# Batch 3 of a sliding-window attention moved into the steady pattern: scores, spread and values in other places of groups 1 and 2

## The chip, the cores and the metric

The kernel runs on one core of a Trainium2 chip. The metric is the device time of one execution in microseconds (us). Five engines take part, each with its own queue of instructions: TensorE (PE), VectorE (DVE), ScalarE (ACT), GpSimd (POOL) and SyncE (SP, which only issues transfers here).

## What is computed

Eight batches of eight heads of causal attention over 576 positions with a window of 128 and a linear distance bias, and then, over all 4608 tokens, a gated feed-forward block:

```python
scores = scale * np.matmul(q, k.transpose(0, 1, 3, 2))
...
mask = (rel >= 0) & (rel < window)
scores = np.where(mask, scores + bias[None], -1000000000.0)
...
attn = np.exp(scores)
attn = attn / (np.sum(attn, axis=-1, keepdims=True) + 1e-09)
return np.matmul(attn, v).astype(np.float32)
...
g = x @ w_gate
gelu = 0.5 * g * (1.0 + erf(g * inv_sqrt2))
val = x @ w_val
return (gelu * val @ w_out).astype(np.float32)
```

The head dimension is 64, the model width 512, the inner width 1536. Inputs and output are float32; the kernel works in bf16 with float32 sums.

## The kernel before

Two kinds of work are woven together. The attention goes batch by batch (`b`, 0 to 7, 576 tokens each), the feed-forward block group by group (`g`, 0 to 8, 512 tokens each). Batch `b` writes its columns of `xT`, the transposed attention output, which the groups read. Group `g` ends at token 512(g+1), so a group needs batches up to `g` or `g + 1`: group 3, tokens 1536 to 2047, needs the end of batch 2 and most of batch 3.

A batch passes through these steps. Heads are taken in four pairs (`c`), the 576 query positions in two parts (`s`, of 320 and 256 columns).

- `load` (L95): GpSimd issues five transfers for each of q, k and v, into `qs`, `ks` and `vb`, of which there are two each (batch parity).
- `transposes_dma` (L167): SP issues two DMA transposes, `kT<-ks` and `qT<-qs`.
- `scores2`, `scores` (L174): products of keys and queries on PE, exponentials on ACT (L181) into `P`, and a product with the mask `emask` on DVE (L184). `scores` works on two of the four head pairs at a time; its exponentials take four PSUM buffers of `ps`.
- `sums` (L232): PE adds up the probabilities with a matrix of ones; DVE takes the reciprocals (L241) into `r`.
- The reciprocals are spread over the partitions into `rb`, in one of two ways. `spread_pe` (L255): four float32 products with a selection matrix on PE for each part, and four copies (L262), two on ACT and two on DVE. `spread_dma` (L245, L247): SP writes `r` to DRAM (`rd`) and reads it back twice with a broadcast (`rb<-rd`).
- `values` (L273): products of values and probabilities on PE; DVE multiplies by `rb` and writes `xT` (L279).

A group has a gate phase of twelve steps `gate_val` (L292, GELU on ACT in L296, product on DVE in L297) and an out phase of eight steps `out_half` (L308), the numbers 0 to 7 in the lists below; the odd ones end with a copy on ACT (L313) and a transfer from SP (L315).

Every engine runs its instructions in the order in which the code issues them. The order is written out by hand: a list `todo[g]` for the out phases of groups 0 to 2, and the function `steps` for the later ones. In the lists, `("s", b, s, cs)` is a call of `scores`, `"s2"` of `scores2`, `"sum"` of `sums`, `"spread"` of `spread_pe`, and `"pv"` of `values`.

In groups 3 to 6 there is a steady pattern for batch `g + 1`: its sums and `spread_dma` come after the first gate step, its values after gate steps 8 and 10; in the out phase, the scores of batch `g + 2` come ahead of and between the products, the last of them ahead of step 6. SP then issues, in the order of the code, rd, two rb, the two transposes of batch `g + 2`, and the four outputs. Batches 0 to 3 are handled in the out phases, with `spread_pe`; batches 2, 3 and 4 are transposed by DMA at the start of groups 1 and 2.

PSUM has eight buffers `ps` of 128x512 float32, from one pool (`bank`), which gate steps, out steps, scores, sums, spreads and values share. `P` has eight buffers for part 0 and four for part 1. `gelu` has three buffers, `r` and `rb` one each.

Of the kernel before, what the change touches and what calls it, by code (L numbers as in the profile page):

```python
# [26 lines left out]
def kernel(  # L27
# [11 lines left out]
    B, H, S, D = q.shape  # L39
# [27 lines left out]
    def bank():  # L67
        ps = psum.tile([128, 512], FP32, name="ps")
        for _ in range(heat.pop()):
            nc.tensor.matmul(out=ps, lhsT=zeros[:, 0:128], rhs=zeros, start=True, stop=True)  # L70
        heat.append(0)
        return ps
# [26 lines left out]
    def load_qk(b):  # L99
        load(qs[b % 2], q, b)  # L100
        load(ks[b % 2], k, b)
# [18 lines left out]
    def load_v(b):  # L120
        load(vb[b % 2], v, b)
# [28 lines left out]
    def transpose(b, what, c, copy):  # L150
        ps = bank().bitcast(BF16)
        for j in range(5):
            nc.tensor.transpose(  # L153
                out=ps[:, 128 * j:128 * j + 128],
                in_=(qs, ks)[what][b][:, j, 128 * c:128 * c + 128], identity=ident)
        copy(out=(qT, kT)[what][b][:, :, c, :],  # L156
             in_=ps[:, 0:640].rearrange("p (j t) -> p j t", t=128))
# [7 lines left out]
    def transposes_dma(b):  # L165
        for src, dst in ((ks, kT), (qs, qT)):
            nc.sync.dma_start_transpose(  # L167
                out=dst[b % 2].rearrange("p j c t -> p (j c) t"),
                in_=src[b % 2].rearrange("p j x -> p (j x)"))
# [49 lines left out]
    def prob(b, s, c, i, j, n):  # L219
        if (s, j) == (0, 2):  # L220
            return probs2[b][:, c, i, 0:n]
        return probs[b, s, c][:, i, PCOL[s][j]:PCOL[s][j] + n]
# [3 lines left out]
    def sums(b, s):  # L226

        ps = bank()
        for j, a, e in PIECES[s]:
            for i in (0, 1):  # L230
                for c in range(4):
                    nc.tensor.matmul(  # L232
                        out=ps[32 * c:32 * c + 32, a:e],
                        lhsT=ones[:, min(j, 1), i, :], rhs=prob(b, s, c, i, j, e - a),
                        start=(i == 0 and j == 2 * s), stop=(i == 1 and j == 2 * s + 2),
                        skip_group_check=True)
        if s == 0:
            sumrow[b] = r_pool.tile([128, S], FP32, name="r")
            recip[b] = r_pool.tile([128, 4, S], FP32, name="rb")
        lo, hi = PART[s]  # L240
        nc.vector.reciprocal(sumrow[b][:, lo:hi], ps[:, 0:hi - lo])  # L241

    def spread_dma(b):
        d = d_pool.tile([4, 2, S], FP32, name="rd")
        nc.sync.dma_start(out=d.rearrange("c i s -> (c i) s"), in_=sumrow[b][0:128:16, :])  # L245
        for i in (0, 1):
            nc.sync.dma_start(  # L247
                out=recip[b][64 * i:64 * i + 64, :, :],
                in_=d[:, i, :].unsqueeze(0).to_broadcast((64, 4, S)))
# [14 lines left out]
    def values(b, s, cs):  # L264
        lo, hi = PART[s]
        pss = []
        for c in cs:
            ps = bank()
            pss.append(ps)
            for j, a, e in PIECES[s]:  # L270
                for i in (0, 1):
                    h = 2 * c + i
                    nc.tensor.matmul(  # L273
                        out=ps[64 * i:64 * i + 64, a:e],
                        lhsT=vb[b % 2][:, j, 64 * h:64 * h + 64],
                        rhs=prob(b, s, c, i, j, e - a),
                        start=(j == 2 * s), stop=(j == 2 * s + 2), skip_group_check=True)
        for c, ps in zip(cs, pss):
            nc.vector.tensor_tensor(  # L279
                out=xT[:, c, b * S + lo:b * S + hi], in0=ps[:, 0:hi - lo],  # L280
                in1=recip[b][:, c, lo:hi], op=ALU.mult)
# [3 lines left out]
    def gate_val(g, f, lo=0, hi=512):  # L285
        if g not in hid:
            hid[g] = h_pool.tile([128, NF, 512], BF16, name="hT")
        t0 = 512 * g
        pg, pv = bank(), bank()
        for w, ps in ((wg, pg), (wv, pv)):  # L290
            for c in range(4):
                nc.tensor.matmul(  # L292
                    out=ps[:, 0:hi - lo], lhsT=w[:, c, 128 * f:128 * (f + 1)],
                    rhs=xT[:, c, t0 + lo:t0 + hi], start=(c == 0), stop=(c == 3))
        gl = g_pool.tile([128, 512], BF16, name="gelu")
        nc.scalar.activation(out=gl[:, 0:hi - lo], in_=pg[:, 0:hi - lo], func=AF.Gelu)  # L296
        nc.vector.tensor_tensor(out=hid[g][:, f, lo:hi], in0=pv[:, 0:hi - lo],  # L297
                                in1=gl[:, 0:hi - lo], op=ALU.mult)
# [3 lines left out]
    def out_half(g, u):  # L302
        t, half = u // 2, u % 2
        if half == 0:
            acc[g] = bank()
        po = acc[g]
        for f in range(6 * half, 6 * half + 6):
            nc.tensor.matmul(  # L308
                out=po, lhsT=hid[g][:, f, 128 * t:128 * (t + 1)],
                rhs=wo[:, f, :], start=(f == 0), stop=(f == NF - 1))  # L310
        if half == 1:
            osb = o_pool.tile([128, DM], FP32, name="osb")
            nc.scalar.copy(out=osb, in_=po)  # L313
            r0 = 512 * g + 128 * t
            nc.sync.dma_start(out=out[r0:r0 + 128, :], in_=osb)  # L315
# [93 lines left out]
    for t in (qs[0], ks[0]):  # L409
# [11 lines left out]
        1: [("s2", 2), ("s", 2, 0, (0, 1)), 0, ("s", 2, 0, (2, 3)), 1, 2,  # L421
            ("s", 2, 1, (0, 1), lambda: sums(2, 0)), 3, ("s", 2, 1, (2, 3)), ("s2", 3),
            ("spread", 2, 0), ("pv", 2, 0), 4, ("sum", 2, 1), ("s", 3, 0, (0, 1)), 5, 6,
            ("spread", 2, 1), ("pv", 2, 1), ("s", 3, 0, (2, 3)), 7],
        2: [("s", 3, 1, (0, 1), lambda: sums(3, 0)), 0, ("s", 3, 1, (2, 3)), 1,
            ("spread", 3, 0), ("pv", 3, 0), ("s2", 4), ("sum", 3, 1), 2,
            ("s", 4, 0, (0, 1)), 3, ("spread", 3, 1), ("pv", 3, 1), 4, ("s", 4, 0, (2, 3)), 5,
            ("s", 4, 1, (0, 1)), 6, 7, ("s", 4, 1, (2, 3))],
    }

    def steps(g):
        b = g + 2
        if g in todo:
            return todo[g]
        if b >= B:
            return range(8)
        return [("s2", b), ("s", b, 0, (0, 1)), 0, 1, ("s", b, 0, (2, 3)), 2, 3,
                ("s", b, 1, (0, 1)), 4, 5, ("s", b, 1, (2, 3)), 6, 7]

    RUN = {"s2": scores2, "s": scores, "sum": sums, "spread": spread_pe,  # L440
           "pv": lambda b, s: values(b, s, range(4))}

    for g in range(NG):
        for b in ((), (2, 3), (4,))[g] if g < 3 else ():
            transposes_dma(b)
        if g + 2 < B:
            load_v(g + 2)
        for f in range(3 if g == 0 else 0, NF):
            gate_val(g, f)
            if g == 0 and f >= 8:  # L450
                for w in (0, 1):
                    transpose(1, w, f - 8, (act, dve)[w])
            if 3 <= g < B - 1:
                if f == 0:
                    sums(g + 1, 0)
                    sums(g + 1, 1)
                    spread_dma(g + 1)
                    if g + 2 < B:
                        transposes_dma(g + 2)
                elif f in (8, 10):  # L460
                    for s in (0, 1):
                        values(g + 1, s, (f - 8, f - 7))
        if g + 3 < B:
            load_qk(g + 3)
        for item in steps(g):
            if isinstance(item, int):
                out_half(g, item)
            else:
                RUN[item[0]](*item[1:])
# [30 lines left out]
```

The softmax here doesn't subtract the row's maximum and nothing guards it: scores larger than these inputs give would overflow.

## Time and profile before

| | |
|---|---|
| time, median of 4 runs | 366.95 us (366.79 to 367.12) |
| profiled execution: time, span | 367.12 us, 365.4 us |
| PE busy | 351.3 us, 96% |
| DVE, ACT, POOL busy | 189.0, 187.3, 107.9 us |
| granted PE clock | 1.00 |
| gate phase of group 2 begins, by the PE timeline | 111.36 us |
| out phase of group 2 begins | 132.17 us |
| gate phase of group 3 begins | 151.57 us |
| gate phase of group 4 begins | 189.56 us |

The span is the time from the first to the last recorded instruction. Rows of the profile name the engine, the line of the kernel, the operation and, as out<-in, what it writes and reads; a row of a timeline starts with its start and its duration in us. PEld is the load of weights, which overlaps PE. SPq and POOLq are the queues from which SP and GpSimd issue transfers. Matmuls are pipelined, so the sum of their durations is no measure of how near PE is to its peak; the chain of waits tells what the end depended on.

### The profile page before, as it was taken

To read this page: it belongs to the slowest core of one execution; us is meant where nothing else is said; L and a number is where in the kernel's file an instruction comes from. 1 tells how busy PE (TensorE), PEld (TensorE's weight loads), DVE (VectorE), ACT (ScalarE), POOL (GpSimd) and SP (SyncE) were. 2 spreads that over 40 slices of the span, in tenths; PEclk is the share of its full clock that TensorE was granted. 3 is DMA by queue.
4 is the path that set the end of the run, shared out by engine and by line. 5 is a ranking of instruction groups with operands and counts; after the bars stand their busy time and mean duration, and the time that the engine had idled before them with its cause. 6 is when DMAs were issued, how large, how long until landed. Compare 5 with 4: busy or idle time off the path is not lost.

```text
span 365.4 us, 6652 instructions
## 1 busy us (share of the span) xinstructions
PE 351.3 (96%) x2638; PEld 170.7 (47%) x2682; DVE 189.0 (52%) x307; ACT 187.3 (51%) x339; POOL 107.9 (30%) x140
## 2 busy tenths in 40 slices
PE   7889999999999999999999999999999999999995
PEld 2455545444454445444544444444444444444442
DVE  4794448533795469474537554755564404302320
ACT  4953487435966376933783277436842223323321
POOL 8945869904419203900940040000000000000000
PEclk9999999999999999999999999999999999999999
DMA  9999999999989994999992992093205030011002
GB/s 103 138 200 178 183 157 188 175 160 201 142 120 122 132 96 81 154 101 227 112 198 45 220 104 90 31 216 58 88 31 131 0 111 5 0 60 58 0 31 86
DMA packets 151168, 41.41 MB, mean 113 GB/s; under 512 B 138816, under 2 KB 144448, under 8 KB 151136
## 3 DMA queue, kind: packets, MB, share of 16 engines
q0 software_dynamic: 112608, 18.88, 68.0%
q1 hardware_dynamic: 38528, 22.10, 27.8%
q8 instruction: 21, 0.34, 0.4%
q14 instruction: 11, 0.09, 0.1%
HBM read 42.47 MB, written 9.51 MB: 142 GB/s over the span
## 4 chain that ended last, share of the span: by engine, by line
PE 83%; ACT 6%; DMA 6%; DVE 2%; issue 1%; POOL 0%; SPq 0%; ACTq 0%; DVEq 0%; POOLq 0%
PE ps L292 48%; PE ps L308 23%; ACT P L181 5%; DMA qT<-qs 5%; PE ps L174 4%; PE ps L273 4%; PE ps L232 2%; PE ps L255 1%; DMA ks<-in_k_dram 1%; DVE xT L279 1%; DVE P L184 1%; PE ps L153 1%; DVE r L241 0%; ACT L181 0%; PE ps L70 0%
## 5 line engine op out<-in xcount | busy, mean ns | idle before, releaser
L297 DVE TENSOR_TENSOR hT<-ps,gelu 128x512 bf16<-128x512 f32 (+2 forms) x111 | 74.4, 674 | 121.6 <-PE ps L292 106.9
L296 ACT ACTIVATE gelu<-ps 128x512 bf16<-128x512 f32 (+2 forms) x111 | 64.9, 585 | 119.8 <-PE ps L292 119.7
L292 PE MATMUL ps<-xT,wg 128*128 128x512 bf16 (+2 forms) x430 | 110.9, 373 | 1.7 <-DVE xT L279 0.7
L292 PE MATMUL ps<-xT,wv 128*128 128x512 bf16 (+2 forms) x435 | 110.4, 373 | 0.6
L308 PE MATMUL ps<-wo,hT 128*128 128x512 bf16 x413 | 97.2, 380 | 1.5 <-issue 0.6
L181 ACT ACTIVATE P<-ps 128x512 bf16<-128x512 f32 x144 | 74.4, 633 | 7.1 <-PE ps L174 7.0
L292 PEld LDWEIGHTS <-wv 128*128 128x128 bf16 x444 | 43.3, 98 | 50.5 <-issue 0.5
L292 PEld LDWEIGHTS <-wg 128*128 128x128 bf16 x444 | 41.9, 98 | 49.8 <-issue 2.3
L184 DVE TENSOR_TENSOR P<-P,emask 128x1024 bf16<-128x1024 bf16 x72 | 48.3, 685 | 31.3 <-ACT P L181 31.0
L308 PEld LDWEIGHTS <-hT 128*128 128x128 bf16 x432 | 39.8, 98 | 49.0 <-issue 4.4
L95 POOL DMA_DIRECT2D vb<-in_v_dram x40 | 33.7, 869 | 77.4 <-PE ps L273 77.2
L313 ACT COPY osb<-ps 128x512 f32<-128x512 f32 x36 | 21.7, 603 | 37.5 <-PE ps L308 33.0
L95 POOL DMA_DIRECT2D qs<-in_q_dram x35 | 29.6, 884 | 24.7 <-DMA qT<-qs 13.0
L241 DVE RECIPROCAL r<-ps 128x320 f32<-128x320 f32 (+1 forms) x16 | 30.7, 1937 | 2.6 <-PE ps L232 2.6
L95 POOL DMA_DIRECT2D ks<-in_k_dram x35 | 29.7, 898 | 4.5 <-DMA wv<-in_moe_w_val_dram 1.6
L174 PE MATMUL ps<-qT,kT 64*128 64x256 bf16 (+1 forms) x384 | 23.3, 245 | 1.9 <-DVE kT L156 0.4
L279 DVE TENSOR_TENSOR xT<-ps,rb 128x320 bf16<-128x320 f32 (+1 forms) x64 | 24.7, 447 | 0.5 <-PE ps L273 0.3
L174 PEld LDWEIGHTS <-kT 64*128 64x128 bf16 x384 | 13.0, 94 | 16.7 <-issue 12.4
L273 PE MATMUL ps<-P,vb 128*64 128x128 bf16 (+2 forms) x384 | 18.4, 243 | 0.1
L273 PEld LDWEIGHTS <-vb 128*64 128x64 bf16 x384 | 14.7, 110 | 6.8 <-issue 6.8
L232 PE MATMUL ps<-P,ones 128*32 128x128 bf16 (+2 forms) x384 | 10.8, 243 | 1.3 <-DVE P L184 1.1
L232 PEld LDWEIGHTS <-ones 128*32 128x32 bf16 x384 | 7.9, 96 | 5.5 <-issue 4.7
(50 smaller groups left out, 98.2 us busy)
## 6 DMA issues: line engine op xcount, KB each, us to landing
out_dram<-osb SPq DMA_DIRECT2D x36, 256.0 KB, 2.5
rb<-rd SPq DMA_DIRECT2D x8, 576.0 KB, 7.5
vb<-in_v_dram POOLq DMA_DIRECT2D x32, 128.0 KB, 5.6
qs<-in_q_dram POOLq DMA_DIRECT2D x28, 128.0 KB, 6.6
ks<-in_k_dram POOLq DMA_DIRECT2D x28, 128.0 KB, 6.4
wg<-in_moe_w_gate_dram POOLq DMA_DIRECT2D x4, 384.0 KB, 10.7
wv<-in_moe_w_val_dram POOLq DMA_DIRECT2D x4, 384.0 KB, 11.9
wo<-in_moe_w_out_dram POOLq DMA_DIRECT2D x2, 768.0 KB, 10.7
```

What stands on the lines that cost most here:

```text
L95: nc.gpsimd.dma_start(out=t[lo:128, j, :].rearrange("p (h d) -> p h d", h=H), in_=src[b][:, 128 * j - 64 + lo:128 * j + 64, :].rearrange(" ...
L174: nc.tensor.matmul(out=ps[:, col:col + 128 * n].rearrange("p (n t) -> p n t", n=n), lhsT=blocks(kT, b, i, c, j, 1).rearrange("p n t -> p ( ...
L181: nc.scalar.activation(out=dst, in_=src, func=AF.Exp, scale=0.125)
L184: nc.vector.tensor_tensor(out=dst, in0=dst, in1=m, op=ALU.mult)
L232: nc.tensor.matmul(out=ps[32 * c:32 * c + 32, a:e], lhsT=ones[:, min(j, 1), i, :], rhs=prob(b, s, c, i, j, e - a), start=(i == 0 and j == ...
L241: nc.vector.reciprocal(sumrow[b][:, lo:hi], ps[:, 0:hi - lo])
L273: nc.tensor.matmul(out=ps[64 * i:64 * i + 64, a:e], lhsT=vb[b % 2][:, j, 64 * h:64 * h + 64], rhs=prob(b, s, c, i, j, e - a), start=(j == ...
L279: nc.vector.tensor_tensor(out=xT[:, c, b * S + lo:b * S + hi], in0=ps[:, 0:hi - lo], in1=recip[b][:, c, lo:hi], op=ALU.mult)
L292: nc.tensor.matmul(out=ps[:, 0:hi - lo], lhsT=w[:, c, 128 * f:128 * (f + 1)], rhs=xT[:, c, t0 + lo:t0 + hi], start=(c == 0), stop=(c == 3))
L296: nc.scalar.activation(out=gl[:, 0:hi - lo], in_=pg[:, 0:hi - lo], func=AF.Gelu)
L297: nc.vector.tensor_tensor(out=hid[g][:, f, lo:hi], in0=pv[:, 0:hi - lo], in1=gl[:, 0:hi - lo], op=ALU.mult)
L308: nc.tensor.matmul(out=po, lhsT=hid[g][:, f, 128 * t:128 * (t + 1)], rhs=wo[:, f, :], start=(f == 0), stop=(f == NF - 1))
```

## The change

Batch 3 takes another way through groups 1 and 2. The last half of its scores, `("s", 3, 1, ...)`, which stood ahead of and behind the first product of group 2, stands at the end of group 1, after that group's last product. Its sums move from group 2's out phase into the gate phase of group 2, after the first and the second gate step, and its reciprocals are spread by `spread_dma` in place of the two `spread_pe`. The two DMA transposes of batch 4 are issued at the start of group 2, as before, so they now stand ahead of batch 3's rd and rb on SP. In group 2's out phase the scores of batch 4 come first, and batch 3's values follow in two halves of two head pairs each: after product 3 and after product 5. The last scores of batch 4 go ahead of product 7. The condition for `transposes_dma` is written in another form and is true for the same groups, 3 to 5.

```diff
@@ todo
         1: [("s2", 2), ("s", 2, 0, (0, 1)), 0, ("s", 2, 0, (2, 3)), 1, 2,
             ("s", 2, 1, (0, 1), lambda: sums(2, 0)), 3, ("s", 2, 1, (2, 3)), ("s2", 3),
             ("spread", 2, 0), ("pv", 2, 0), 4, ("sum", 2, 1), ("s", 3, 0, (0, 1)), 5, 6,
-            ("spread", 2, 1), ("pv", 2, 1), ("s", 3, 0, (2, 3)), 7],
-        2: [("s", 3, 1, (0, 1), lambda: sums(3, 0)), 0, ("s", 3, 1, (2, 3)), 1,
-            ("spread", 3, 0), ("pv", 3, 0), ("s2", 4), ("sum", 3, 1), 2,
-            ("s", 4, 0, (0, 1)), 3, ("spread", 3, 1), ("pv", 3, 1), 4, ("s", 4, 0, (2, 3)), 5,
-            ("s", 4, 1, (0, 1)), 6, 7, ("s", 4, 1, (2, 3))],
+            ("spread", 2, 1), ("pv", 2, 1), ("s", 3, 0, (2, 3)), 7, ("s", 3, 1, (0, 1)),
+            ("s", 3, 1, (2, 3))],
+        2: [("s2", 4), ("s", 4, 0, (0, 1)), 0, 1, ("s", 4, 0, (2, 3)), 2, 3,
+            ("pv", 3, 0, (0, 1)), ("pv", 3, 1, (0, 1)), 4, ("s", 4, 1, (0, 1)), 5,
+            ("pv", 3, 0, (2, 3)), ("pv", 3, 1, (2, 3)), 6, ("s", 4, 1, (2, 3)), 7],
@@ RUN
-           "pv": lambda b, s: values(b, s, range(4))}
+           "pv": lambda b, s, cs=range(4): values(b, s, cs)}
@@ the loop over groups
-            if 3 <= g < B - 1:
+            if 2 <= g < B - 1:
                 if f == 0:
                     sums(g + 1, 0)
+                if f == (1 if g == 2 else 0):
                     sums(g + 1, 1)
                     spread_dma(g + 1)
-                    if g + 2 < B:
+                    if 2 < g < B - 2:
                         transposes_dma(g + 2)
-                elif f in (8, 10):
+                elif g > 2 and f in (8, 10):
                     for s in (0, 1):
                         values(g + 1, s, (f - 8, f - 7))
```

## The prediction

> **What bounds the kernel now.** I read the page first: busy times, then the chain that ended last.
>
> ```profile
> PE 351.3 (96%) x2638; PEld 170.7 (47%) x2682; DVE 189.0 (52%) x307; ACT 187.3 (51%) x339; POOL 107.9 (30%) x140
> PE 83%; ACT 6%; DMA 6%; DVE 2%; issue 1%; POOL 0%; SPq 0%; ACTq 0%; DVEq 0%; POOLq 0%
> ```
>
> The matmul engine is on the chain for 83% of the span; ACT and DVE are half idle. So the change counts by the matmuls it removes and by the waits of PE it ends or makes. Next, the chain in order of time, for groups 1 to 3:
>
> ```profile
> 111.52 9.71 PE ps L292 x45
> ...
> 136.75 0.75 PE ps L255 x8
> ...
> 142.84 0.66 PE ps L255 x8
> ...
> 151.65 2.08 ACT P L181 x4
> 153.76 0.70 DVE P L184
> 154.50 0.60 PE ps L232 x21
> ```
>
> Group 2 runs from 111.5 us to 151.6 and is almost pure PE. The two L255 rows are batch 3's spread: 0.75 and 0.66 us of PE. At 151.65 the chain leaves PE: the last exponentials of batch 4, issued after group 2's last product, hold up batch 4's sums; the PE timeline puts the gap at 0.37 us ("idle before" of the L232 row at 154.50). Third, the timelines of ACT and of the SP queue, which the moved steps join:
>
> ```profile
> 109.91 2.06 ACT L181 ACTIVATE P<-ps 128x512 bf16<-128x512 f32 x4 [0.70 <-PE ps L174]
> 111.83 0.62 ACT L313 COPY osb<-ps 128x512 f32<-128x512 f32 x1
> 112.47 1.28 ACT L296 ACT_TABLE_LOAD   x1
> ```
>
> ```profile
> 121.61 7.95 SPq L167 DMA_TRANSPOSE qT<-qs  x1
> 137.85 14.26 SPq L315 DMA_DIRECT2D out_dram<-osb  x4
> 160.06 0.71 SPq L245 DMA_DIRECT2D rd<-r  x1
> 161.94 1.32 SPq L247 DMA_DIRECT2D rb<-rd  x2
> 163.49 6.62 SPq L167 DMA_TRANSPOSE kT<-ks  x1
> 170.27 3.06 SPq L167 DMA_TRANSPOSE qT<-qs  x1
> ```
>
> ACT is busy up to group 2's start (at 112.47 it only loads a table), so more exponentials there queue up. On SP, batch 4's transposes are issued long before batch 4's scores, which now start at 138.6. Group 3 shows the order that batch 3 will now take in group 2: rd, rb, rb, but there with the transposes behind them.
>
> [...] a row of L255 takes 479 or 426 ns, yet all eight take 0.75 and 0.66 us. I use the chain's times, not count by mean. [...] beside GpSimd's loads (queue q0) SP's transposes (q1) move 1049 packets in 131 to 134 us, alone 5071 in 169 to 175:
>
> ```profile
> q1 hardware_dynamic: 1049, 0.26, 65.3%
> q0 software_dynamic: 917, 0.12, 58.4%
> ```
>
> ```profile
> q1 hardware_dynamic: 5071, 1.28, 111.2%
> ```
>
> The columns are packets, MB and share of the window: 350 packets per us against 845. [...] the trace shows the same 1283. The new order keeps the number of switches, so it costs nothing more.
>
> **The change part by part.** I write F for the start of a group's first gate product.
>
> 1. Removed: `spread_pe(3, 0)` and `(3, 1)`. PE loses 0.75 + 0.66 = **1.41 us**, all on the path. ACT and DVE lose four copies each (about 0.44 us each, off the path).
>
> 2. `scores(3, 1)` to the end of group 1: the same 24 matmuls, so no PE time in itself (two runs of 0.55 us), but ACT is behind. Buffers, from the order of the instructions and their waits: the last of the eight `ps` needed is the one that out 7 leaves when its copy ends, 111.83 + 0.62 = 112.45. Unhindered the scores would run 111.4 to 112.5; the last six matmuls (0.27 us) now end near 112.75: 0.25 lost. The first gate product needs the buffer of the first new exponential: ACT is free at about 112.3 (neighbours overlap), plus 0.63 makes 112.94: 0.2 lost. Eight exponentials in a row take 4.03 us (the ACT row at 133.32), so the last ends at 116.35 and its mask (0.69) at 117.05. `sums(3, 1)` after gate product 1 is reached at 112.95 + 1.73 + 0.60 + 1.73 = 117.0: 0.1 lost. Together **0.55 us, 0.3 to 1.2**. GELU 0 comes at 117.65 behind the table load; its buffer is next wanted at 119.4. The two reciprocals (2.15 and 1.72 us) end at 121.0 and 123.3 on DVE, their buffers are wanted at 122.8 and 125.4. So nothing more.
>
> 3. `sums(3, *)` inside the gate products: the same 48 matmuls, nothing.
>
> 4. Batch 4's scores first in group 2's out phase. They need the qT transpose of batch 4. F is 112.95, the gate products take 20.8 and the sums 1.2, so PE asks at 135.0 instead of 138.6. SP issues that transpose from 121.61 to 129.56 in both kernels, with the same loads beside it; in 134 to 137 us the DMA engines are almost idle (5 GB/s), so it has landed by about 134. Slack 1 us: **nothing**, at worst 1.1.
>
> 5. `spread_dma(3)` puts three DMAs on SP behind both transposes of batch 4 and ahead of group 2's four outputs. r is ready at 123.3, but rd goes out after 129.6, and its packets behind the transposes, at about 134. From rd's issue group 3 needs about 1.9 us to the first rb and 7.1 to 8.1 more to landing: rb at about 143; no row shows an rd behind transposes, so 142 (its packets mix in) to 145 (it waits for all of them and starts slowly), and I take 143. The values of batch 3 (same 48 matmuls for two halves of 1.06 us) are on PE at 141.9; DVE then waits up to 1 us for rb. What hides it: PE has out 4 and scores to run, and first needs a buffer that DVE holds at 144.7. The outputs behind on SP wait for nothing, the first copy coming near 139. **Nothing**; at the late end 0.3 us, and 1 us only if rb lands near 145.7.
>
> 6. `("s", 4, 1, (2, 3))` now ahead of out 7: its exponentials end about 1.3 us before the sums of batch 4. The gap of **0.37 us** goes, as in group 4, where the same order shows no wait there.
>
> 7. GpSimd's queue: load_v(5) waits for the last values of batch 3, now near 147.0 instead of 144.6 (two of five loads at 138.75). Its fifteen loads at 0.845 us end at 159.9 instead of 155.6, and their packets near 163 instead of 159.5. Batch 5's transposes in group 3 come after this; **nothing**, see the first rival.
>
> Sum: -1.41 - 0.37 + 0.55 = **-1.2 us**. The profiled execution took 367.12 (span 365.4), the slowest of the four shown; 365.9 on its base. Their median is 366.95, 0.17 below, so **365.75**, written 365.8. About 0.2% (0.73 us) is what a measurement of this kernel can tell from no change.
>
> **Rivals.**
>
> *Batch 5's transposes land late (slower).* In group 3, rd goes out at F + 7.15 (group 4: 189.56 to 196.72). F is now 150.7, so rd at 157.9, 2.2 us earlier than before, while the loads end 4 us later: they overlap rd and rb, perhaps the transposes. From rd to qT landed, undisturbed: 15.1 us (group 3), 17.2 (group 4), 15.7 (group 5), so 173.0 to 175.1; the scores of batch 5 ask at F + 24.5 = 175.2. The slack of 0.1 to 2.2 us is all there is. If transposes suffer as batch 4's did beside loads (8.41 + 7.95 us on the queue against 6.62 + 3.06), they are 6.7 us later: a wait of 4.5, net +3.3, 370.3. It decides from a landing after 177.1, that is a wait over 1.9 us. Against it: rb goes first, [...]; the loads should be through by the time the transposes start near 166. Chance 0.17.
>
> *Batch 4's transposes are late (no change).* If they land at 136 instead of 134, PE stands still for 1 us at group 2's first scores, and the gain shrinks to 0.1 to 0.4: about 366.7. For it: only 1 us of slack. Chance 0.15.
>
> *The new wait takes the old one's place (no change).* rb lands after 144.7, or the queue of exponentials at group 1's end costs its upper bound of 1.2: gain 0.6 or less, about 366.4. Chance 0.08.
>
> That the spread stays on PE is excluded: in the instruction order the eight L255 rows of batch 3 are gone.
>
> **How the numbers follow.** Forecast 0.60, its own range 365.4 to 366.2: the junction from 0.3 to 1.0. The low end of the whole range, 365.0, is the junction at nothing with group 4's wait of 0.17 gone as well. Upwards it takes in both no-change rivals and the mild part of the first, to 367.6; what is left out is most of the 0.17 and a little below. Faster 0.60, within 0.2% 0.23, slower 0.17.
>
> **What would show it.** Right: the chain without L255 after 110 us; the gate products of group 2 starting near 113.0, those of group 3 near 150.7; no L232 wait after group 3's first product; xT waiting under 1 us for rb in group 2. Wrong: an idle time of PE "<-DMA qT<-qs" over 0.5 us at the start of the out phase of group 2 or 3, an L292 row in group 2 waiting for ACT over 1 us, or PE waiting for xT.

## The result and the profile after

| | before | after |
|---|---|---|
| median | 367.06 us (55 runs) | 368.47 us (35 runs) |
| lowest to highest | 366.51 to 368.15 | 365.69 to 372.19 |
| after / before, 95% interval | | 1.0033 (1.0022 to 1.0045) |

The changed kernel is slower by 0.33%, 1.2 us, where 1.2 us of gain was forecast. It also scatters over 6.5 us where the kernel before scatters over 1.6. The ratio leaves out two slow executions of the changed kernel (371.84 and 372.19 us), which the medians, 1.4 us apart, count.

The profiled execution of the changed kernel took 365.69 us (span 363.9), and that is the fastest of all 35. Read alone, it would confirm the forecast. First the busy times and the shares of the chain, from its page:

```profile
PE 349.7 (96%) x2622; PEld 170.0 (47%) x2666; DVE 187.4 (51%) x303; ACT 186.0 (51%) x335; POOL 107.9 (30%) x140
PE 85%; ACT 7%; DMA 3%; DVE 2%; issue 1%; SPq 0%; POOL 0%; ACTq 0%; DVEq 0%; POOLq 0%
```

PE has 1.6 us less to do, as the two spreads were to give. The chain of waits in order of time (start, duration, what) shows what became of the places that the prediction named:

```profile
112.49 0.66 ACT P L181
113.15 0.04 issue
113.19 1.89 PE ps L292 x8
...
142.15 1.06 PE ps L273 x24
...
150.97 1.73 PE ps L292 x8
152.70 1.05 PE ps L232 x48
...
170.37 4.96 DMA qT<-qs
175.33 0.14 issue
175.47 0.84 PE ps L174 x16
```

There is no L255 row after 110 us; group 2's gate phase waits a moment for the exponentials of batch 3 and begins at 113.19; the sums in group 3 stand directly behind the products at 152.70. New is the row at 170.37: the chain leaves PE for batch 5's qT transpose, 5 us long. In the timeline of PE it costs little in this execution:

```profile
175.47 0.84 PE L174 MATMUL ps<-qT,kT 64*128 64x128 bf16 x16 [0.29 <-DMA qT<-qs]
```

0.29 us, where before the same row had no wait:

```profile
176.46 0.83 PE L174 MATMUL ps<-qT,kT 64*128 64x128 bf16 x16
```

How near that is to more shows in the timeline of the SP queue:

```profile
127.77 0.71 SPq L245 DMA_DIRECT2D rd<-r  x1
134.42 1.32 SPq L247 DMA_DIRECT2D rb<-rd  x2
...
158.26 0.61 SPq L245 DMA_DIRECT2D rd<-r  x1
162.12 1.25 SPq L247 DMA_DIRECT2D rb<-rd  x2
163.59 6.62 SPq L167 DMA_TRANSPOSE kT<-ks  x1
170.37 3.12 SPq L167 DMA_TRANSPOSE qT<-qs  x1
```

Group 3's rd goes out 1.8 us earlier than before (160.06), as worked out. But the first rb follows 3.86 us after it and not 1.88, and so the two transposes start no earlier than before (163.49 and 170.27), while PE, which wants them, comes over 1 us earlier (it asks at 175.18; before, its chain row for these scores stands at 176.53). rb may only be read once rd has landed. The summary of the SP queue's waits has this wait for all groups together (total, number, longest); before it read 4.4, 4, 1.1:

```profile
SPq L247 <- DMA rd<-r: 12.4, 5, 5.9
```

Most of this rise of 8.0 us is batch 3's own read-back in group 2, which is new on this queue and has the longest wait, 5.9 us; about 2 us of it are group 3's.

What stands beside rd here is seen in the DMA queues of 159 to 161 us in this trace (packets, MB, share of the window; q0 is GpSimd's queue):

```profile
q0 software_dynamic: 2376, 0.30, 234.6%
```

These are the loads of v5, q6 and k6, which GpSimd could not issue before batch 3's values were done, now near 147 instead of 144.6. No packet of q1, SP's queue, moves in these 2 us: rd's first packet starts at 161.10, and the last one of the loads at 164.00. In the kernel before the last packet of the loads started at 160.37, and rd's first at 161.36, so the two missed each other by 1 us.

### The profile page after: what moved, and what is told of

Read it like the earlier page. It is cut to its first block, busy times and chain, and to the rows that moved or that the text cites. A ratio compares the mean times of both kernels' runs of the same rounds, so it can differ in the third digit from the quotient of the medians.

```text
span 363.9 us, 6614 instructions
## 1 busy us (share of the span) xinstructions
PE 349.7 (96%) x2622; PEld 170.0 (47%) x2666; DVE 187.4 (51%) x303; ACT 186.0 (51%) x335; POOL 107.9 (30%) x140
## 4 chain that ended last, share of the span: by engine, by line
PE 85%; ACT 7%; DMA 3%; DVE 2%; issue 1%; SPq 0%; POOL 0%; ACTq 0%; DVEq 0%; POOLq 0%
PE ps L292 50%; PE ps L308 23%; ACT P L181 6%; PE ps L273 4%; PE ps L174 4%; PE ps L232 2%; DMA ks<-in_k_dram 1%; DMA qT<-qs 1%; DVE xT L279 1%; PE ps L255 1%; ACT L181 1%; DVE P L184 1%; PE ps L153 1%; DVE r L241 0%; PE ps L70 0%
## 5 line engine op out<-in xcount | busy, mean ns | idle before, releaser
L232 PE MATMUL ps<-P,ones 128*32 128x128 bf16 (+2 forms) x384 | 10.6, 243 | 0.9 <-DVE P L184 0.7
L232 PEld LDWEIGHTS <-ones 128*32 128x32 bf16 x384 | 7.9, 96 | 5.6 <-issue 4.4
```

The costliest lines, as they stand in the source:

```text
L232: nc.tensor.matmul(out=ps[32 * c:32 * c + 32, a:e], lhsT=ones[:, min(j, 1), i, :], rhs=prob(b, s, c, i, j, e - a), start=(i == 0 and j == ...
```

## The experiments

The theory from this trace: the new order is worth what was forecast, and the loads of v5, q6 and k6, now beside group 3's rd, take it back through a late rd, late transposes and a wait of PE at group 3's out phase. The rivals: the loss comes from another place (the junction at the end of group 1, the way of batch 3 through SP), or the loads have no part in it.

**look1, look2: the changed kernel again, for two more traces.** No edit.

> The changed kernel once more, for a trace of one of its slower executions (the median is 368.5, the one traced so far took 365.7). Theory L (the loads of v(5), q(6), k(6), which start at 147 instead of 138.8 and 144.6, collide with rd, rb and the transposes of batch 5 in group 3): in an execution of 368 or more, PE waits 2 to 4 us for qT at the start of group 3's out phase, near 175. Theory G2 (batch 4's transposes, or batch 3's rd and rb behind them, land late in group 2): PE waits there, near 135 or 144 to 147, instead. Theory C (the granted clock alone): no wait, but matmuls at less than full clock somewhere.

> As the look before, a second sample: the same place of the wait if one mechanism is behind it, another place if there are two.

366.71 and 366.73 us; from rd to the first rb 4.20 and 4.15 us. The timeline of PE in look1:

```profile
176.48 0.84 PE L174 MATMUL ps<-qT,kT 64*128 64x128 bf16 x16 [1.83 <-DMA qT<-qs]
```

1.83 us of waiting here, 1.76 in look2, at the same place and for the same tile as the 0.29 above. Both executions were 0.5 us ahead when rd went out (157.73 and 157.82 against 158.26), so the wait, 1.5 us longer, makes the spans 1.0 and 1.1 us longer (364.9 and 365.0 against 363.9). Neither was one of the executions of 368 us or more for which they were meant; look3, further down, is one.

**loads_late: the q6 and k6 loads behind the next v.** The loads of q and k for batches 6 and 7 are issued after those of v6 and v7, so that nothing but v5 is loaded at 147 us.

```diff
         if g + 2 < B:
             load_v(g + 2)
+        if 4 <= g < B - 2:
+            load_qk(g + 2)
...
-        if g + 3 < B:
+        if g < 3:
             load_qk(g + 3)
```

> The changed kernel with one thing moved: q(6), k(6) are loaded after v(6), and q(7), k(7) after v(7), so that only five of the fifteen loads are left ahead of group 3's rd. Theory L: the spread of times goes, all executions 365 to 366, ratio to before about 0.996. Theory G2: as the changed kernel, 366 to 371, ratio 1.003. Theory C: the same, 1.003.

365.45 us, ratio 0.9963 (0.9950 to 0.9975). The SP queue:

```profile
157.73 0.61 SPq L245 DMA_DIRECT2D rd<-r  x1
159.56 1.25 SPq L247 DMA_DIRECT2D rb<-rd  x2
```

1.83 us, and in group 3 PE waits for no transfer. All else of the change is in this kernel; so the change without this collision is a gain, about the size of the forecast.

**before_late: the same edit on the kernel before.**

> The kernel before with the same edit as loads_late (q(6), k(6) after v(6), q(7), k(7) after v(7)). If loads_late's gain is only the collision that it takes away, this changes nothing, since the kernel before had none: 366.6 to 367.2, ratio 0.999 to 1.001, and 366.9 less 365.45, some 1.4 us, is what the rest of the change is worth. If late loads are worth something by themselves (groups 4 and 5), it is faster than before by 0.5 us or more.

366.81 us, ratio 0.9993 (0.9984 to 1.0002). The edit is worth nothing by itself: rd to the first rb is 1.87 us with it (160.39, 162.26), as it is without. It helps only where the collision is.

**qk_first: q6 and k6 ahead of v5.** The loads of q6 and k6 don't need batch 3's values; v5 does.

```diff
         if g + 2 < B:
+            if g == 3:
+                load_qk(6)
             load_v(g + 2)
...
-        if g + 3 < B:
+        if g + 3 < B and g != 3:
             load_qk(g + 3)
```

> The changed kernel with the loads of q(6), k(6) ahead of v(5): they no longer stand behind the values of batch 3 and start when batch 4's transposes land, near 133, so group 3's rd at 158 has only v(5) ahead, done by 153. Theory L: no wait near 175. But now the loads lie beside rd and rb of batch 3 in group 2: if small packets delay rd there as they do in group 3 (4.2 us to rb instead of 1.9), rb lands 2 us later, near 144.5, and PE waits up to 1 us near 145 to 147: 365.2 to 366.6. Without such a delay 365.2 to 365.8.

365.28 us, ratio 0.9946 (0.9929 to 0.9963), the lowest median of all, though five executions each don't tell it from loads_late. The same edit on the kernel before was not run. rd 158.21, rb 160.05. In 159 to 161 us the DMA queues now show rd alone:

```profile
q1 hardware_dynamic: 16, 0.02, 3.0%
```

The 16 packets are rd's: eight of 2304 bytes and eight of 4. In this trace the first starts 1.24 us after rd's issue. In look1 the first starts 2.68 us after it (160.41), and the last 1.14 us after the first, against 0.21. So most of the delay lies ahead of rd's first data packet.

**before_held, after_later: the loads held back on purpose.** A small GpSimd copy of a late tile of P goes ahead of the loads, into a tile `hold` that nothing reads: the first line below in the kernel before, the second in the changed one.

```diff
         if g + 2 < B:
+            if g == 3:
+                nc.gpsimd.tensor_copy(out=hold, in_=probs[4, 0, 3][:, 0, 0:64])  # before_held
+                nc.gpsimd.tensor_copy(out=hold, in_=probs[4, 1, 2][:, 0, 0:64])  # after_later
             load_v(g + 2)
```

> The kernel before with one thing added: ahead of v(5), q(6), k(6) GpSimd copies 64 columns of a P tile of batch 4 that is masked near 149, so that these fifteen loads start near 149.4 instead of 138.8 and 144.6 and end near 162, about 2 us after group 3's rd goes out at 160. Theory L: the slowness of the changed kernel appears without any of its reordering: rd to rb takes 3 to 5 us instead of 1.9, PE waits 0.5 to 3 us for qT near 176, 367.5 to 370. If another part of the change does it (G2, or the order of the products): as before, 366.9.

> The changed kernel with the suspected cost enlarged: the loads of v(5), q(6), k(6) held by a GpSimd copy of a P tile masked near 151.2, so that they run from 151.4 to 164 instead of 147.3 to 160. Theory L: rb goes out later still, part of the transposes run beside the loads, PE waits 3.5 to 6 us for qT near 175 in the traced execution, which takes 368.5 to 371; if long waits lower the granted clock, it is below 1 after 178. G2 or C: as the changed kernel traced so far, a wait of 0.3 to 1.8.

before_held: 371.61 us, 1.0124 (1.0083 to 1.0164). The kernel before, with nothing of the change but late loads, becomes slow, even beyond the 370 us expected, and its PE timeline has the same wait:

```profile
178.37 0.84 PE L174 MATMUL ps<-qT,kT 64*128 64x128 bf16 x16 [2.19 <-DMA qT<-qs]
```

rd to rb took 3.69 us, and 3.4 us at half clock follow the wait. after_later, with the loads at 151.75: 373.97 us, 1.0187 (1.0167 to 1.0207). There the loads, issued until 164.32, reach into the transposes themselves:

```profile
162.13 1.26 SPq L247 DMA_DIRECT2D rb<-rd  x2
163.61 10.12 SPq L167 DMA_TRANSPOSE kT<-ks  x1
...
182.51 1.46 PE L174 MATMUL ps<-qT,kT 64*128 64x128 bf16 x16 [5.88 <-DMA qT<-qs]
```

The kT transpose takes 10.12 us on the queue instead of 6.62. The wait is in the range expected; the time, 374.13 us in the traced execution, is 3 us over it, and the clock is halved for 6.83 us here. That is the rival of the prediction in full; the changed kernel itself never got so far.

**held_1us: the same with about 1 us.** The copy reads `probs[4, 1, 1]`.

> The changed kernel with the loads of v5, q6 and k6 held about 1 us longer, behind a small GpSimd copy of 64 columns of the third tile of P(4,1) pair 1. Theory (loads beside the write and read-back of group 3, and a half-clock stretch where the wait passes about 2 us): the loads start at 148.2 to 148.8 and end at 163.5; the first read-back follows its write by 3.9 to 4.3 us; TensorE waits 2 to 3.5 us for qT near 177, followed by about 3.4 us at half clock; 368 to 371 us. Rival (the time of the changed kernel does not hang on when these loads run): 366.7 to 368.5 as the changed kernel itself.

368.49 us, 1.0041 (1.0024 to 1.0058); the loads began at 148.16, 0.8 us later than in the profiled execution of the changed kernel (147.32), rd to rb took 3.80, PE waited 2.31 us, with 3.4 us at half clock behind it. By its time, which lies in both ranges, it can't be told from the changed kernel: inconclusive. The load of q6 and k6 was already beside all of rd.

**look3, look4: the changed kernel twice more.**

> The changed kernel, once more. Theory: write to first read-back 3.7 to 4.3 us, a wait of TensorE of 0.3 to 3 us for qT near 176.5; a stretch at half clock only where that wait is over about 2 us, and then a span some 3 us longer than in the execution with a wait of 0.29. Rival (the slower executions come from elsewhere): a long span beside a short wait there.

> The same again, with the same expectation: write to first read-back 3.7 to 4.3 us, a wait of 0.3 to 3 us near 176.5, half clock only behind a wait of over about 2 us, and the span following from these two.

368.57 and 367.44 us. The PE timelines of look3, then look4:

```profile
176.64 1.47 PE L174 MATMUL ps<-qT,kT 64*128 64x128 bf16 x16 [2.01 <-DMA qT<-qs]
```

```profile
177.22 0.83 PE L174 MATMUL ps<-qT,kT 64*128 64x128 bf16 x16 [2.32 <-DMA qT<-qs]
```

In look3 the same 16 products take 1.47 us instead of 0.84. The view by stretches (length, busy time of the engines, then PEclk, the granted clock; DMA share; GB/s) of look3 and of look1 shows why:

```profile
176.00:178.00 2.00, 1.36 (x16) 0.95 (x16) 0.00 (x0) 0.75 (x2) 1.67 (x3) 0.67 2.31 147
178.00:180.00 2.00, 1.78 (x6) 0.74 (x6) 1.34 (x2) 2.00 (x5) 2.00 (x3) 0.50 2.32 154
180.00:182.00 2.00, 2.00 (x14) 0.84 (x14) 0.74 (x2) 0.47 (x2) 2.00 (x4) 0.98 2.28 142
```

```profile
176.00:178.00 2.00, 1.52 (x20) 0.99 (x21) 0.00 (x0) 1.11 (x3) 1.85 (x3) 1.00 2.34 149
178.00:180.00 2.00, 2.00 (x12) 0.75 (x12) 1.42 (x3) 1.94 (x4) 2.00 (x3) 1.00 2.12 141
```

In look3 PE has half its clock from about 176.7 to 180.1, and does 6 products in 178 to 180 us where look1 does 12. The clock is halved for 3.41 us, so about 1.7 us of work are lost on top of the wait. The whole group shows the same sum: from group 3's first gate product to group 4's it is 41.10 us in look3 and 37.39 in loads_late, 3.71 more, which is the wait of 2.01 and 1.70. The expectation that only the wait's length decides (over about 2 us) did not hold: look4 waited 2.32 us and kept its clock.

What goes with the half clock shows when the record of the granted clock in the traces is laid over PE's idle time. In the profiled execution of the changed kernel the clock is full for 358.399 us and half behind the last product, in that of the kernel before full for 361.813: 105 and 106 times 3.4133 us. In the other traces, too, every stretch at full clock that ends in half clock lasts a whole multiple of this (50, 51, 54, 55, 105 or 106 times). So the changes recorded in one trace lie on a grid of 3.413 us; where the grid lies differs from execution to execution (these two stretches begin 4.36 and 4.77 us into the span). The windows of this grid around the wait:

| trace | wait of PE | idle PE in the windows it touches | clock in the next window |
|---|---|---|---|
| look2 | 1.76 | 1.76 | full |
| look1 | 1.83 | 1.81 | full |
| look4 | 2.32 | 1.59, then 0.78 | full, full |
| before_held | 2.19 | 0.2, then 1.97 | full, half |
| look3 | 2.01 | 2.01 | half |
| held_1us | 2.31 | 2.31 | half |
| after_later | 5.88 | 2.09, then 3.41, then 0.37 | half, half, full |

look4's wait was split over two windows, with 1.59 and 0.78 us of it. In the 1690 whole windows of the sixteen traces there is no exception: where PE was idle for up to 1.81 us the next one is at full clock, where it was idle for 1.97 or more at half. Nothing in between was seen, and no run tells why it is so.

**What still differed.** The five traces of the changed kernel agree in rd to rb within 0.34 us (3.86 to 4.20), yet the waits go from 0.29 to 2.32. The second difference is in the list of transfers: the median time from issue to landing of the qT transpose, in the profiled execution of 365.69 us and in look1.

```profile
qT<-qs SPq DMA_TRANSPOSE x1, 5.0
```

```profile
qT<-qs SPq DMA_TRANSPOSE x1, 6.1
```

It took 6.0 and 6.4 us in look3 and look4. The queues of look1 in 175 to 176 us:

```profile
q0 software_dynamic: 826, 0.10, 163.0%
q1 hardware_dynamic: 32, 0.00, 4.4%
```

The transposes' data are through by then; their last 32 packets, of 4 bytes each, run beside the load of v6, whose first packets came in 174 to 175 us. In the execution of 365.69 us these 32 packets went in 174 to 175 us, and 175 to 176 held none of q1. It is a matter of tenths: there the load's first packet started at 174.91, after the last of the 32 (174.80); in look1 at 174.69, just after the transposes' last data (174.63) and ahead of most of the 32, the last of which started at 175.98. look2 to look4, held_1us and before_held are as look1 in this, and landed after 6.0 to 6.4 us.

**v6_behind: the load of v6 kept away from the end of the transposes.** q7 overwrites a tile that the transposes of batch 5 read, so its load can't start before they have landed; put ahead of v6's, it holds that one too. v5, q6 and k6 stay as in the changed kernel.

```diff
         if g + 2 < B:
+            if g == 4:
+                load_qk(7)
             load_v(g + 2)
...
-        if g + 3 < B:
+        if g + 3 < B and g != 4:
             load_qk(g + 3)
```

> The changed kernel with load_qk(7) ahead of load_v(6): the first load of q7 overwrites a tile that batch 5's transposes read, so no load runs before these have landed; v5, q6 and k6 are loaded as in the changed kernel. Theory of two parts (the write and read-back of group 3 are 2 us later because of v5, q6, k6; then the end of the transposes meets the first packets of v6's load, which holds back the landing by another 1.1 us): write to first read-back still 3.8 to 4.2 us, qT landing 5.0 us after its issue and not 6.0 to 6.4, a wait of TensorE of 0.3 to 0.8 us near 176, no half-clock stretch, and 365.6 to 366.3 us, ratio 0.996 to 0.998. Rival (v6's loads have no part in it): waits of 1.8 to 2.3 us, half clock in half of the executions, 367.5 to 369 us.

> The same kernel, for a second trace: write to first read-back 3.8 to 4.2 us, qT landing about 5.0 us after its issue, a wait of 0.3 to 0.8 us, no half clock. Rival: a landing of 6 us or more, and a wait of 1.8 us or more.

366.41 us, ratio 0.9985 (0.9975 to 0.9996), and 365.61 in the second traced execution. rd to rb 4.35 and 3.85 us; the qT transpose landed 4.9 us after its issue in both; the waits of PE are 1.23 and 0.22. The SP queue and PE in the first trace:

```profile
158.19 0.61 SPq L245 DMA_DIRECT2D rd<-r  x1
162.54 1.25 SPq L247 DMA_DIRECT2D rb<-rd  x2
```

```profile
176.33 0.84 PE L174 MATMUL ps<-qT,kT 64*128 64x128 bf16 x16 [1.23 <-DMA qT<-qs]
```

The wait of 1.23 is above the 0.8 expected, as rd to rb took 4.35 us here, and the median is 0.1 us above its range; the landing is as expected, and of the 14 executions 13 have a mean granted clock of 0.998 or more. The rival (v6 has no part in it) falls: the late rd and the late landing are two losses, told apart by this kernel.

**pe_spread: batch 3's spread given back to PE,** in group 2's out phase, the rest of the change left.

```diff
-        2: [("s2", 4), ("s", 4, 0, (0, 1)), 0, 1, ("s", 4, 0, (2, 3)), 2, 3,
+        2: [("s2", 4), ("s", 4, 0, (0, 1)), 0, 1, ("s", 4, 0, (2, 3)), 2,
+            ("spread", 3, 0), 3, ("spread", 3, 1),
...
-                    spread_dma(g + 1)
+                    if g > 2:
+                        spread_dma(g + 1)
```

> The changed kernel with batch 3's reciprocals spread on PE again (two spread_pe in group 2's out phase, no spread_dma there): rd and rb are gone from group 2, 1.4 us of PE come back. Theory G2 with rb as the late one: the spread of times goes, 366.8 to 367.2. Theory L: it stays, since the loads and group 3 are as they were: 367 to 372, ratio 1.005. Theory G2 with the transposes as the late ones, and theory C: it stays as well.

369.12 us, 1.0059 (1.0040 to 1.0079). In its trace group 3's gate phase starts at 152.60 instead of 150.81: of the 1.8 us 1.5 lie in group 2, for the two spreads (0.75 and 0.64 to the next row), the rest ahead of it. PE waits only 0.24 us for qT in this execution of 367.91 us; the slower ones have no trace. Its rd met the loads as well (3.84 us to rb). So batch 3's own way through SP is not what costs the time.

**best: another list for group 1, on top of qk_first.** Batch 3's scores are spread between products 5, 6 and 7.

```diff
-            ("spread", 2, 0), ("pv", 2, 0), 4, ("sum", 2, 1), ("s", 3, 0, (0, 1)), 5, 6,
-            ("spread", 2, 1), ("pv", 2, 1), ("s", 3, 0, (2, 3)), 7, ("s", 3, 1, (0, 1)),
+            ("spread", 2, 0), ("pv", 2, 0), 4, ("sum", 2, 1), ("s", 3, 0, (0, 1)), 5,
+            ("s", 3, 0, (2, 3)), 6, ("spread", 2, 1), ("pv", 2, 1), ("s", 3, 1, (0, 1)), 7,
```

> The version with load_qk(6) ahead of load_v(5) (365.28 us in its own comparison, 0.9946), and group 1's list put so that batch 3's scores are not its last four parts: s(3,0) before and after product 5, product 6, then spread(2,1) and pv(2,1), s(3,1) half 1, product 7, s(3,1) half 2. If the junction costs the 0.3 to 0.6 us at which the prediction had it, most of that goes: the gate phase of group 2 starts 0.3 to 0.5 us earlier than 113.19, and the time is 364.7 to 365.2, ratio about 0.994. Theory that the junction is hidden or merely moved: 365.3 as before it. In both, the first read-back of group 3 follows its write by 1.8 to 2 us, and TensorE has no wait for a transposed tile in the output phase.

365.86 us, 0.9986 (0.9973 to 0.9998): a miss, and slower than qk_first. Group 2's gate phase starts at 113.31, not earlier; from group 1's first gate product it comes after 44.73 us, and after 44.16 in qk_first. A new wait came up in group 1:

```profile
110.39 1.04 PE L174 MATMUL ps<-qT,kT 64*128 64x128 bf16 x12 [0.39 <-DVE rb L262]
```

The junction's cost was moved, not removed. This span (363.7) is 0.2 above that of qk_first (363.5); why its median is 0.6 above was not followed up.

## Why the prediction was right and wrong

1. *The spread leaves PE.* Right: no L255 after 110 us, 1.6 us less of PE (forecast 1.41).
2. *The junction, 0.55 us.* Right. Group 2's gate phase begins at 113.19 (predicted 112.95), but the whole execution shifts by up to 0.5 us from trace to trace. From group 1's first gate product it is 44.16 us in the first trace and in look1 to look4 within 0.01, and 42.52 before: 1.64 more, of which 1.10 are the moved products, 0.54 the loss. That moving the scores can save it was not shown. The table loads on ACT are 14 of 1283 ns in both kernels.
3. *Batch 4's transposes and rb(3).* Right: group 2's out phase takes them at 135.4 without a wait; rd went out at 127.77, ahead of the 129.6 forecast, with its first packet at 133.04, after the transposes' last data at 132.13 (the order was an estimate of the author's), and the first rb at 134.42, and DVE begins batch 3's values at 142.70 without waiting. The second and third rivals did not come.
4. *The L232 wait of 0.37 us.* Gone, as predicted.
5. *Group 3 begins at 150.7.* 150.81 in the trace. With the collision taken out, loads_late and qk_first stand at 0.9963 and 0.9946, 1.4 and 2.0 us below their runs of before (forecast 1.2). In their traces, from group 1's first gate product to the end, both are 1.98 us shorter than before: 0.95 by the start of group 3 (forecast 0.86), 0.60 in group 3 (forecast 0.37) and 0.43 after it, where the forecast had nothing. So, for a kernel in which step 7 holds, the sum held up to the start of group 3 and was too small from there on.
6. *Step 7, the loads: "nothing".* This is the step that failed. The prediction had the loads end 4 us later and overlap rd; the profile shows just that. It set their cost to nothing because rb goes first and the loads should be through when the transposes start. That looks at rb and at the transposes. What the loads hold back is rd, one small write that must land before rb may be issued at all: 3.86 to 4.20 us instead of 1.83 to 1.88. The "1.9 us from rd to the first rb" was carried over from groups in which no load runs beside rd. In its place PE waited 0.29 to 2.32 us for qT in the five traces, where the step had nothing.
7. *The first rival (0.17).* Right in its place, its sign and its turning point: a wait of more than 1.9 us was said to make the change slower. The traces with 1.76 and 1.83 us took 366.7, about the time before; that with 2.32 took 367.44. Wrong in its way: the transposes were not slowed by loads beside them (kT took 6.6 to 7.2 us on the queue); they started 2 us late and their landing came 1.1 us late. Its weight was too small for a slack of 0.1 to 2.2 us.
8. *In none of the cases: the clock.* The prediction priced a wait of PE at its bare length. Of the 35 executions of the changed kernel, 18 have a mean granted clock of 0.998 or more and a median of 367.16 us; 17 have 0.995 or less and a median of 369.6. One 3.41-us stretch at half clock in 367 us makes 0.9954. In look3 it cost 1.7 us on top of the wait. That the rest of the 2.4 us is longer waits is likely but not shown: of all traces of the changed kernel look3 alone has such a stretch ahead of its last product.

The balance. Group 3, from its first gate product to group 4's, takes 37.39 us in loads_late and qk_first, 37.75 to 41.10 in the five traces of the changed kernel. In the medians, against each kernel's own runs of before: the change with neither meeting 0.9946 to 0.9963; with the late rd alone (v6_behind) 0.9985; with the late landing too (as submitted, 1.0033). So the late rd costs 0.2 to 0.4%, 0.8 to 1.4 us, and the late landing with the half clock seen behind its longer waits 0.5%, 1.8 us. This division takes the edit of v6_behind to be worth nothing by itself; it was not run on the kernel before.

Open is why the start of rd's first packet waits so long behind the loads. Open too are executions that took long at full clock: the changed kernel's up to 369.65 us, pe_spread's up to 370.68, and one of best of 368.38, though its trace has no late rd; none of them was traced.

## What to carry to other kernels

A moved step also moves what queues behind it: when the values of a batch go later, the loads that wait for their buffers go later, and the question is which small, serial transfer they will then run beside. A write that must land before the next transfer may start is to be priced under the load that will be there: rd to rb took 3.86 to 4.20 us here instead of 1.83 to 1.88. And where a wait of 2.01 us is followed by half clock in one trace (look3) and one of 2.32 us is not in another (look4), one trace is not enough: the first here was the fastest of 35. Issuing the loads that are free first (qk_first) cost nothing here and made the change the gain that it was meant to be.

## What the runs showed of the hardware

- From the issue of rd, a write of 18 KB to DRAM, to the issue of its first read-back it took 1.8 to 1.9 us in group 3 where no load ran beside it, and 3.7 to 4.4 beside loads in 128-byte packets, at some 1190 packets per us in the profiled execution of the changed kernel. Most of the extra lies ahead of the first data packet, which starts 2.68 us after the issue in look1 and 1.24 in qk_first. Why was not shown.
- qT landed 4.9 to 5.0 us after its issue in the traces (the profiled execution of the changed kernel, v6_behind and its second trace) in which no load of v6 ran beside its last 32 packets of 4 bytes, and 6.0 to 6.4 us after it in those (look1 to look4, held_1us, before_held) in which the load began ahead of most of them. No run here tells why.
- After a wait of PE of 2.01, 2.19 or 2.31 us the clock was halved for 3.41 us, after 5.88 us for 6.83, after 1.76, 1.83 and once 2.32 us not at all. In these traces the clock changed on a grid of 3.413 us, which lies elsewhere in each execution: after a window with 1.97 us or more of idle PE the next one was at half clock, after one with 1.81 us or less at full.
